# Token order by the second exp, whole-tile output transfers, and one batch loaded by half its heads

## The chip, the cores and the metric

The kernel runs on one core of a Trainium2 chip. The metric is device time in microseconds; the time before is 251.23 us, the median of three runs from 250.75 to 251.34. The core has a matrix engine (TensorE, PE in the profile, with its weight loads as PEld), a vector engine (VectorE, DVE), an activation engine (ScalarE, ACT), GpSimd (POOL) and SyncE (SP). POOL and SP issue most of the transfers here. Matrix results land in PSUM; everything else on the chip lies in SBUF.

## The reference

Eight batches, eight heads, 576 tokens, head size 64. A short set p of 32 rows a head attends to all keys and values; its result, the packed rows, serves as keys and as values for the queries. Then comes a two-layer network on the 4,608 tokens.

```python
def _attn_ref(q, k, v, p):
    scale = 1.0 / np.sqrt(q.shape[-1])
    def sm_attn(qq, kk, vv):
        s = scale * np.matmul(qq, kk.transpose(0, 1, 3, 2))
        s = s - np.max(s, axis=-1, keepdims=True)
        a = np.exp(s)
        a = a / (np.sum(a, axis=-1, keepdims=True) + 1e-09)
        return np.matmul(a, vv)
    p_packed = sm_attn(p, k, v)
    return sm_attn(q, p_packed, p_packed)

def _moe_ref(x, w_in, w_out):          # x: (4608, 512), w_in: (512, 2048), w_out: (2048, 512)
    h = x @ w_in
    g = np.where(h >= 1, h, np.where(h <= -1, 0.0, (h + 1) ** 2 / 4))
    return g @ w_out
```

## The kernel before

**Steps of a batch.** The names in brackets are the profile's. k and q are loaded with 96 partitions, each holding six successive tokens: token 6p + c lies in partition p, place c. c is written as 2e + x, with e from 0 to 2 and x 0 or 1. Both are turned, so that head size and x lie in the partitions and the columns run over e and then p. Batches 0 to 2 are turned by PE and an eviction (`trans`: tp, kT, qT), batches 3 to 7 by DMA transposes in SP's queue (`turned`, L512). Scores of p against k (`scores`: sp) go through an exp (ex), then products with v and sums (`packed`: pk), whose evictions (p, ppT, rs) leave the packed rows and the reciprocal sums. Queries against packed rows (`weights`: s) go through the second exp (eT, L456); its column sums (sm) are inverted by ln and exp (ln, rc), and DVE multiplies (A, L472). Both matmuls of A and of the hidden layer are merged: the packed rows are multiplied with w_in ahead of time (`mk`: mp, then M by a cast), four quarters a batch, and a hidden tile (`hidden_tile`: h, L548) is M times A, 128 hidden units by 576 tokens, 16 tiles a batch. Three steps on ACT and DVE make the activation (x, then hT). An output tile (`out_tile`: o, L598) is 128 tokens by 512, 16 steps over the hidden units; two batches share nine output tiles. It is evicted (ob) and sent out from SP's queue (L604), the last one in two halves from ACT's and SP's queues (L612).

**The order of tokens.** The columns of A, hT and so of the output tiles run over x, e and p, not in the order of the tokens. `out_rows` cuts a tile where e, x or the batch changes, and each piece goes to every sixth row of the output:

```python
n = min(TP - r, (i + 1) * P - t)
res.append((t - i * P, n, out[b * S:(b + 1) * S].rearrange("(p c) d -> c p d", c=NC)[X * e + x, r:r + n]))
```

**What sets the order of the work.** `Plan` (a list of tasks with costs, keys and dependencies) is run once when the program is written: it plays the engines through with the times in `C` and gives each engine a fixed order. The loads have one order of their own, that in which they were added (POOL's queue). `C["load"]` is the planned time of one load of a batch (288 KB halves cost `half`), and `C["xland"]` what passes between a DMA transpose and its landing. The actual engines then follow that order and wait on semaphores. PSUM has three wide buffers ("W") and two for output tiles ("O"). Until the plan has its first output tiles open, PE's gaps are filled with matmuls on zeros (L661).

**The loads.** Batch 0 comes by halves of the heads; then the four quarters of w_in and of w_out, with batch 1 ahead of the last w_out quarter; then p for the later batches and the batches 2 to 7 in turn. Of batch 1, k and q come in halves and v whole. Packing is done by halves of the heads (two calls of `packed`) in batch 0 alone; in the other batches it is one step for all heads.

Of the kernel before, what the change touches and what calls it, by code (L numbers as in the profile page):

```python
# [8 lines left out]

C = dict(load=2.95, half=1.46, w_in=2.57, w_out=2.57, rest=1.25, out=9.0, p=4.05, land=1.75, xt=5.0, xland=11.0,
         tpp=0.06, tp=0.042, sc=0.034, pk=1.05, s2=0.25, sm=0.245, M=0.345, h=0.49, o=0.217, switch=0.05, join=0.15,
         pTc=0.1, Tca=1.12, Tcd=0.76, ex=0.82, ppT=0.42, ppo=0.41, ppa=0.4, ppd=0.2, rs=0.18, eT=0.74, ln=0.65, rc=0.68, A=0.82,
         Mca=1.0, Mcd=1.22, x=0.65, ta=0.683, td=0.457, hT=0.758, oba=0.585, obd=0.69,
# [17 lines left out]
class Plan:  # L33
# [15 lines left out]
    def add(self, engines, cost, key, deps, fn, takes=None, readers=0, frees=None, mode=None, slack=None, after=0.0,  # L49
            holds=0.0):  # L50
        engines = (engines,) if isinstance(engines, str) else engines
        t = Task(engines, cost if isinstance(cost, dict) else {e: cost for e in engines}, key, deps, fn, takes, readers,
                 frees, mode, slack, after, holds)
        t.seq = len(self.tasks)
        self.tasks.append(t)
        return t
# [124 lines left out]
def kernel(  # L181
# [10 lines left out]
    nc = tc.nc  # L192
    f32 = mybir.dt.float32
    bf16 = mybir.dt.bfloat16
    AF = mybir.ActivationFunctionType
    ALU = mybir.AluOpType

    B, H, S, D = q.shape
# [3 lines left out]
    P = 128  # L202
    assert d_model == H * D and n_tokens == B * S
    assert S == 576 and D == 64 and NP == 32 and H == 8 and d_ff == 2048 and B % 2 == 0
    scale = 1.0 / math.sqrt(D)
# [3 lines left out]
    G = 2  # L209
    Q = 4  # L210
    TP = 96
    NC = S // TP
    X = 2
    E = NC // X
    HALF = S // X
    KF = d_ff // P
    FW = 512
    NF = d_ff // FW
# [15 lines left out]
    PE, ACT, DVE, DMA, SP = "PE", "ACT", "DVE", "DMA", "SP"  # L234
# [42 lines left out]
    def add_load(nm, b, parts=1, deps=(), cost="load"):  # L277
        for i, hs in enumerate([ALL] if parts == 1 else HS):
            L[nm, b, i] = add(DMA, C[cost] / parts, -1, deps, lambda nm=nm, b=b, hs=hs: load(nm, b, hs))
        if parts == 1:  # L280
            L[nm, b, 1] = L[nm, b, 0]

    def add_weights(which, f):
        if which == "in":
            fn = lambda: nc.gpsimd.dma_start(w_in_sb[:, :, f * FW:(f + 1) * FW], w_in_v[:, :, f * FW:(f + 1) * FW])  # L285
        else:
            fn = lambda: nc.gpsimd.dma_start(w_out_sb[:, 4 * f:4 * f + 4], w_out_v[:, 4 * f:4 * f + 4])
        L[which, f] = add(DMA, C["w_" + which], -1, (), fn)
# [8 lines left out]
            load(nm, 0, HS[i])  # L297
    for nm, i in FIRST:
        L[nm, 0, i] = add(DMA, C["half"], -1, (), (lambda: None) if L else first_loads)
    add_weights("in", 0)  # L300
    add_weights("in", 1)
    add_weights("out", 0)
    add_weights("in", 2)
    add_weights("out", 1)
    add_weights("in", 3)
    add_weights("out", 2)
    add_load("k", 1, 2)
    add_load("v", 1, 1)
    add_load("q", 1, 2)
    add_weights("out", 3)  # L310
    L["p"] = add(DMA, C["rest"], -1, (), lambda: nc.gpsimd.dma_start(p_nat[:, PB * 2:], p_v[:, PB * 2:]))


# [43 lines left out]
    def attention(b, key):  # L357
# [46 lines left out]
        def packed(gs, deps):  # L404
            box, ky = {}, key["pk" + str(gs[0])]
            hs, n = slice(Q * gs[0], Q * gs[-1] + Q), Q * len(gs)
            part = 0.55 if len(gs) < G else 1.0

            def mm():
                pk = wide([P, 1024], f32, "pk")  # L410
                vt, ex_ = tok["v", b], ex()
                v_ = box["v"] = pk[:, :n * X * NP].rearrange("p (h y) -> p h y", h=n)
                for g in gs:
                    for a in range(Q):
                        h = head(g, a)
                        for e in range(E):
                            nc.tensor.matmul(v_[:, h - hs.start].rearrange("p (x n) -> p x n", x=X),  # L417
                                             vt[:, h, X * e:X * (e + 1)].rearrange("p c d -> p (c d)"), ex_[:, e, g, :, a],
                                             start=(e == 0), stop=(e == E - 1))
                s_ = box["s"] = pk[:, 512:512 + 2 * len(gs)].rearrange("p (g y) -> p g y", y=2)  # L420
                for i, g in enumerate(gs):
                    for c in range(NC):
                        nc.tensor.matmul(s_[:, i], ex_[:, c // X, g, c % X].rearrange("p a n -> p (a n)"), ones2[:TP],  # L423
                                         start=(c == 0), stop=(c == NC - 1))
            t = add(PE, C["pk"] * len(gs) / G, ky, [L["v", b, g] for g in gs] + deps + old("s2", "M", "A"), mm, takes="W",
                    readers=3, mode=0)
            war = old("s2", "M")

            def odd(eng):
                box["p1"] = att.tile([D, n, NP], f32, tag="p1", name="p1")  # L430
                copy(box["p1"], box["v"][D:, :, NP:])(eng)
            c1 = both(odd, C["ppo"] * part, C["ppo"] * part, ky, [t] + war, frees=t)
            c2 = add(DVE, C["ppT"] * part, ky, [c1] + war, lambda eng: nc.vector.tensor_tensor(
                ppT()[:D, hs], box["v"][:D, :, :NP], box["p1"], ALU.add), frees=t)
            res = [c2, both(lambda eng: copy(ppT()[D:, hs], ppT()[:D, hs])(eng), C["ppa"] * part, C["ppd"] * part, ky, [c2] + war)]
            r = add(DVE, C["rs"], ky, [t] + old("eT", "A"), lambda eng: nc.vector.reciprocal(
                rs()[:, gs[0]:gs[-1] + 1], box["s"]), frees=t)
            return t, res, r
# [4 lines left out]
        def weights(g, deps, r):  # L443
            box, ky, km = {}, key["s2" + str(g)], key["sm" + str(g)]

            def mm():
                s2 = box["s2"] = wide([P, X, FW], f32, "s2")
                for a in range(Q):
                    h = head(g, a)
                    for x in range(X):  # L450
                        nc.tensor.matmul(s2[a * NP:(a + 1) * NP, x, :HALF], pp_of(x, h),  # L451
                                         qT()[x * D:(x + 1) * D, g, h % 4 * E * TP:][:, :E * TP], start=True, stop=True)

            def exp2(eng):
                box["eT"] = att.tile([P, X, HALF], bf16, tag="eT", name="eT")
                nc.scalar.activation(box["eT"], box["s2"][:, :, :HALF], AF.Exp, scale=rs()[:, g, 1:])  # L456

            def mm2():
                sm = box["sm"] = wide([P, X, FW], f32, "sm")
                for x in range(X):  # L460
                    nc.tensor.matmul(sm[:, x, :HALF], onesblk, box["eT"][:, x], start=True, stop=True)  # L461

            def ln(eng):
                box["ln"] = att.tile([P, X, HALF], f32, tag="ln", name="ln", bufs=1)
                nc.scalar.activation(box["ln"], box["sm"][:, :, :HALF], AF.Ln)  # L465

            def inv(eng):
                box["rc"] = att.tile([P, X, HALF], f32, tag="rc", name="rc")
                nc.scalar.activation(box["rc"], box["ln"], AF.Exp, scale=-1.0)  # L469

            def norm(eng):
                nc.vector.scalar_tensor_tensor(A()[:, g], box["eT"], rs()[:, g, :1], box["rc"], ALU.mult, ALU.mult)  # L472
            p_ = K.get((b - 1, "A" + str(g)), [])
            t, j = yield ky, C["s2"], deps + p_, mm
            e_ = add(ACT, C["eT"], ky, [t, r] + p_, exp2, frees=(t, j))
            t2 = add(PE, C["sm"], km, [e_], mm2, takes="W", readers=1, mode=0)
            l_ = add(ACT, C["ln"], km, [t2] + last.get("ln", []), ln, frees=t2)
            i_ = add(ACT, C["rc"], km, [l_] + p_, inv)
            a_ = add(DVE, C["A"], km, [i_] + K.get((b - 2, "h"), []), norm)
            last["ln"] = [i_]  # L480
            K[b, "A" + str(g)] = [a_]
            yield t, e_, a_
# [39 lines left out]
        s1, e1 = scores(1, kc1 + pT_of[b])  # L522
        q0, qc0 = trans("q", 0, qT, old("s2"))
        q1, qc1 = trans("q", 1, qT, old("s2"))
        pk, pc, r = zip(*([packed((0,), [e0]), packed((1,), [e1])] if b == 0 else [packed((0, 1), [e0, e1])] * G))
        K[b, "sc"], K[b, "pk"] = [s0, s1], list(pk)
        K[b, "kt"], K[b, "qt"] = [k0, k1], [q0, q1]
        ws, ms = [weights(g, pc[g] + (qc0, qc1)[g], r[g]) for g in range(G)], [mk(f, pc[0] + pc[1]) for f in range(NF)]
# [44 lines left out]
    def out_rows(pr, i):  # L573
        res, t = [], i * P
        while t < (i + 1) * P:
            b, x, e, r = 2 * pr + t // S, t % S // HALF, t % HALF // TP, t % TP
            n = min(TP - r, (i + 1) * P - t)
            res.append((t - i * P, n, out[b * S:(b + 1) * S].rearrange("(p c) d -> c p d", c=NC)[X * e + x, r:r + n]))
            t += n
        return res  # L580

# [54 lines left out]
    keys = {0: {nm: -1 + 0.01 * i for i, nm in enumerate(names)}}  # L636
    for f in range(1, NF):
        keys[0]["M" + str(f)] = 0.25 * f - 0.12
    order = "kT0 kT1 sc0 qT0 sc1 qT1 pk0 s20 M0 s21 sm0 M1 sm1 M2 M3".split()
    for b in range(1, B):  # L640
        lo, hi = (b - 1 + 0.05, b - 0.05)
        keys[b] = {nm: lo + (hi - lo) * i / len(order) for i, nm in enumerate(order)}
# [49 lines left out]
```

## Time and profile before

| | |
|---|---|
| median of three runs | 251.23 us (250.75 to 251.34) |
| the profiled execution | 250.97 us |
| its span in the profile | 249.2 us |
| PE busy | 234.8 us (94%) |
| DVE, ACT busy | 181.7 us, 182.5 us (73% each) |
| POOL busy | 29.7 us |
| output transfers at L604 | 70, of 192, 128 and 64 KB |
| chain that ended last | PE 76%, DMA 13%, ACT 3% |

The span is what the profile saw between the first and the last event on the core; the device time of the same execution is 1.8 us longer. Busy shares are means over a run whose stages differ: the beginning is fed by loads, the middle and the end are not. A row of the stretches gives start and end, length, then busy time and count of PE, PEld, DVE, ACT and POOL, the granted clock, the mean share of the DMA engines, and GB/s. A row of a timeline gives start, length, engine, line, operation and tiles, and in brackets the idle time ahead of it and what ended that. A row of a group gives the line, engine, operation, shapes and count, then busy time and mean ns of one, then idle time ahead of the group. A DMA row gives what was moved, the queue, the size, and the time from issue to landing.

### The profile page before, as it was taken

Reading aid. Unit: us, or ns where it says so; the run is one execution under the profiler, and the core shown is the slowest. Engines: PE = TensorE matmul, PEld = TensorE weight load, DVE = VectorE, ACT = ScalarE, POOL = GpSimd, SP = SyncE. Lnnn points to the kernel's source line nnn. Section 1 sums busy time; section 2 is a strip of 40 time slices with the busy share of each in tenths; the row PEclk is TensorE's granted clock in tenths of the full one; section 3 lists DMA queues with packets and bytes.
Section 4 is the critical chain, followed back from the end, with each engine's and each line's share of the span. In section 5 each row is a group of like instructions: output and inputs, shape, how many; then the busy total and the mean of one; then the engine's idle time right before and its main releaser. Section 6 shows DMA issues by size and latency. Waiting matters only on the chain.

```text
span 249.2 us, 5464 instructions
## 1 busy us (share of the span) xinstructions
PE 234.8 (94%) x2187; PEld 140.9 (57%) x2220; DVE 181.7 (73%) x308; ACT 182.5 (73%) x294; POOL 29.7 (12%) x44
## 2 busy tenths in 40 slices
PE   7887887999999999999999999999999999999993
PEld 5655465467546666556565656656556465544452
DVE  5456979788999899698979985998569878930000
ACT  3368888899888899798798984997859796841110
POOL 8632433012001301111101000000000000000000
PEclk9999999999999999999999999999999999999999
DMA  6999999999999999999999932312112112133223
GB/s 99 196 207 207 206 203 195 204 240 204 193 182 217 165 190 193 208 183 188 223 191 223 218 76 53 79 42 49 42 42 45 43 42 45 42 84 86 54 74 84
DMA packets 54825, 34.37 MB, mean 138 GB/s; under 512 B 27536, under 2 KB 50320, under 8 KB 54800
## 3 DMA queue, kind: packets, MB, share of 16 engines
q0 software_dynamic: 24672, 18.55, 49.9%
q1 hardware_dynamic: 29968, 15.34, 31.7%
q8 instruction: 17, 0.28, 0.4%
q10 hardware_dynamic: 160, 0.13, 0.2%
q14 instruction: 8, 0.07, 0.1%
HBM read 37.22 MB, written 9.44 MB: 187 GB/s over the span
## 4 chain that ended last, share of the span: by engine, by line
PE 76%; DMA 13%; ACT 3%; POOL 3%; issue 2%; DVE 2%; DVEq 0%; ACTq 0%; POOLq 0%
PE o L598 44%; PE h L548 22%; DMA w_in_sb<-in_moe_w_in_dram 7%; DMA q<-in_q_dram 6%; PE mp L493 3%; PE sp L397 2%; PE pk L417 1%; PE sm L461 1%; PE s L451 1%; PE tp L376 1%; DVE pT L319 1%; POOL w_in_sb L285 1%; ACT eT L456 1%; POOL k L259 1%; PE pk L423 1%
## 5 line engine op out<-in xcount | busy, mean ns | idle before, releaser
L598 PE MATMUL o<-w_out_sb,hT 128*128 128x512 bf16 (+1 forms) x559 | 135.6, 373 | 2.1 <-issue 1.1
L563 DVE SCALAR_TENSOR_TENSOR hT<-x 128x576 bf16<-128x576 f32 x128 | 93.2, 754 | 8.3 <-PE o L598 3.5
L598 PEld LDWEIGHTS <-hT 128*128 128x128 bf16 x592 | 56.1, 98 | 53.7 <-issue 4.8
L553 ACT ACTIVATE x<-h 128x576 f32<-128x576 f32 x128 | 77.2, 653 | 12.1 <-PE h L548 8.3
L548 PE MATMUL h<-A,M 128*128 128x288 bf16 x512 | 76.0, 286 | 1.4 <-ACT M L319 0.5
L548 PEld LDWEIGHTS <-M 128*128 128x128 bf16 x512 | 49.3, 98 | 24.1 <-ACT M L319 1.0
L558 DVE TENSOR_SCALAR x<-x 128x576 f32<-128x576 f32 x84 | 38.5, 459 | 11.8 <-ACT x L553 10.9
L319 ACT COPY ob<-o 128x512 f32<-128x512 f32 (+1 forms) x23 | 13.2, 576 | 32.1 <-PE o L598 32.1
L560 ACT ACTIVATE x<-x 128x576 f32<-128x576 f32 x44 | 29.4, 683 | 0.5
L319 DVE COPY ob<-o 128x512 f32<-128x512 f32 (+1 forms) x14 | 9.4, 669 | 25.8 <-PE o L598 25.7
L319 DVE CAST M<-mp 128x1024 bf16<-128x1024 f32 x16 | 19.4, 1218 | 2.8 <-PE mp L493 2.8
L319 ACT CAST M<-mp 128x1024 bf16<-128x1024 f32 x16 | 15.8, 1012 | 1.2 <-PE mp L493 1.2
L400 ACT ACTIVATE ex<-sp 96x768 bf16<-96x768 f32 x16 | 12.9, 806 | 3.2 <-PE sp L397 3.1
L472 DVE SCALAR_TENSOR_TENSOR A<-eT,rs,rc 128x576 bf16<-128x576 bf16 x16 | 13.0, 812 | 2.1 <-ACT rc L469 2.1
L259 POOL DMA_DIRECT2D k<-in_k_dram x10 | 7.5, 746 | 56.5 <-DMA kT<-k 40.0
L456 ACT ACTIVATE eT<-s,rs 128x576 bf16<-128x576 f32 x16 | 11.2, 736 | 2.8 <-PE s L451 2.6
L493 PE MATMUL mp<-w_in_sb,ppT 64*32 64x512 bf16 x256 | 10.7, 381 | 2.6 <-DMA w_in_sb<-in_moe_w_in_dram 2.2
L465 ACT ACTIVATE ln<-sm 128x576 f32<-128x576 f32 x16 | 10.4, 648 | 2.2 <-PE sm L461 2.1
L661 PE MATMUL o<-zeros 128*128 128x256 bf16 x68 | 10.6, 301 | 1.2 <-DVE zeros L247 1.2
L469 ACT ACTIVATE rc<-ln 128x576 f32<-128x576 f32 x16 | 10.9, 683 | 0.5
L259 POOL DMA_DIRECT2D q<-in_q_dram x10 | 7.6, 759 | 26.2 <-DMA qT<-q 12.7
L397 PEld LDWEIGHTS <-kT 128*128 128x128 bf16 x192 | 7.4, 98 | 2.6 <-DVE kT L319 0.6
(47 smaller groups left out, 114.4 us busy)
## 6 DMA issues: line engine op xcount, KB each, us to landing
out_dram<-ob SPq DMA_DIRECT2D x23, 192.0 KB, 2.5
v<-in_v_dram POOLq DMA_DIRECT2D x7, 576.0 KB, 18.4
k<-in_k_dram POOLq DMA_DIRECT2D x6, 576.0 KB, 12.4
q<-in_q_dram POOLq DMA_DIRECT2D x6, 576.0 KB, 14.0
out_dram<-ob SPq DMA_DIRECT2D x24, 128.0 KB, 2.8
w_in_sb<-in_moe_w_in_dram POOLq DMA_DIRECT2D x4, 512.0 KB, 14.7
w_out_sb<-in_moe_w_out_dram POOLq DMA_DIRECT2D x4, 512.0 KB, 16.8
out_dram<-ob SPq DMA_DIRECT2D x23, 64.0 KB, 2.0
```

The lines of the kernel that those rows point to most:

```text
L259: nc.gpsimd.dma_start(tok[nm, b][:, hs].rearrange("p h c d -> p h (c d)"), SRC[nm][b, hs].rearrange("h (p c) d -> p h (c d)", c=NC))
L319: return lambda eng: nc.vector.tensor_copy(out_, in_) if eng == DVE else nc.scalar.copy(out_, in_)
L400: nc.scalar.activation(ex()[:, :, i].rearrange("p e x a n -> p e (x a n)"), box["sp"], AF.Exp, scale=scale)
L456: nc.scalar.activation(box["eT"], box["s2"][:, :, :HALF], AF.Exp, scale=rs()[:, g, 1:])
L472: nc.vector.scalar_tensor_tensor(A()[:, g], box["eT"], rs()[:, g, :1], box["rc"], ALU.mult, ALU.mult)
L493: nc.tensor.matmul(mp[a * NP:(a + 1) * NP, g], pp_of(y, h), w_in_sb[y * D:(y + 1) * D, h // 2, f * FW:(f + 1) * FW], start=True, stop=True)
L548: nc.tensor.matmul(h[:, hf, :HALF], T[b, "M"][:, g, fi * P:(fi + 1) * P], T[b, "A"][:, g, hf], start=(g == 0), stop=(g == G - 1))
L553: nc.scalar.activation(box["x"], box["h"][:, :, :HALF], AF.Prelu, bias=-1.0, alpha=0.5)
L558: nc.vector.tensor_scalar(x, x, 1.0, 0.0, ALU.add, ALU.max)
L560: nc.scalar.activation(x, x, AF.Relu, bias=1.0)
L563: nc.vector.scalar_tensor_tensor(hT[:, fi, col:col + S].rearrange("p (a t) -> p a t", a=2), box["x"], 1.0, box["x"], ALU.min, ALU.mult)
L598: nc.tensor.matmul(o, hT[:, fi, i * P:(i + 1) * P], w_out_sb[:, fi, cs], start=(fi == 0), stop=(fi == KF - 1))
```

## The change

Four things are changed. First, the second exp writes its result in the order of the tokens in all batches: it reads PSUM as before and writes each value six elements from the one before it. So A, hT and the output tiles are in token order, and an output tile goes out as one transfer, or two where it holds the end of one batch and the beginning of the next. Second, v of batch 1 is loaded by halves of the heads as well, and the order of the loads between batch 0 and p is changed: three quarters of w_in, two of w_out, the first halves of k and v, the second half of k, the last quarter of w_in, the second half of v, the third quarter of w_out, both halves of q, the last quarter of w_out. Third, batch 1 is packed by halves of the heads like batch 0, and the list of keys has a place for the second half. Fourth, two planned times are changed: a load is 2.7 in place of 2.95, the landing of a transpose 18 in place of 11.

```diff
-C = dict(load=2.95, half=1.46, w_in=2.57, w_out=2.57, rest=1.25, out=9.0, p=4.05, land=1.75, xt=5.0, xland=11.0,
+C = dict(load=2.7, half=1.46, w_in=2.57, w_out=2.57, rest=1.25, out=9.0, p=4.05, land=1.75, xt=5.0, xland=18.0,
...
+    ORDERED = range(B)
...
-    add_weights("in", 0)
-    add_weights("in", 1)
-    add_weights("out", 0)
-    add_weights("in", 2)
-    add_weights("out", 1)
-    add_weights("in", 3)
-    add_weights("out", 2)
-    add_load("k", 1, 2)
-    add_load("v", 1, 1)
-    add_load("q", 1, 2)
-    add_weights("out", 3)
+    for nm in "i0 i1 i2 o0 o1 k0 v0 k1 i3 v1 o2 q0 q1 o3".split():
+        if nm[0] in "io":
+            add_weights({"i": "in", "o": "out"}[nm[0]], int(nm[1]))
+        else:
+            i = int(nm[1])
+            L[nm[0], 1, i] = add(DMA, C["half"], -1, (), lambda nm=nm, i=i: load(nm[0], 1, HS[i]))
...
-                nc.scalar.activation(box["eT"], box["s2"][:, :, :HALF], AF.Exp, scale=rs()[:, g, 1:])
+                eT, s2 = box["eT"], box["s2"][:, :, :HALF]
+                if b in ORDERED:
+                    eT = eT.rearrange("p y t -> p (y t)").rearrange("p (t e x) -> p x e t", x=X, e=E)
+                    s2 = s2.rearrange("p x (e t) -> p x e t", e=E)
+                nc.scalar.activation(eT, s2, AF.Exp, scale=rs()[:, g, 1:])
...
-        pk, pc, r = zip(*([packed((0,), [e0]), packed((1,), [e1])] if b == 0 else [packed((0, 1), [e0, e1])] * G))
+        pk, pc, r = zip(*([packed((0,), [e0]), packed((1,), [e1])] if b < 2 else [packed((0, 1), [e0, e1])] * G))
...
-            n = min(TP - r, (i + 1) * P - t)
-            res.append((t - i * P, n, out[b * S:(b + 1) * S].rearrange("(p c) d -> c p d", c=NC)[X * e + x, r:r + n]))
+            if b in ORDERED:
+                n = min(S - t % S, (i + 1) * P - t)
+                res.append((t - i * P, n, out[b * S + t % S:][:n]))
+            else:
+                n = min(TP - r, (i + 1) * P - t)
+                res.append((t - i * P, n, out[b * S:(b + 1) * S].rearrange("(p c) d -> c p d", c=NC)[X * e + x, r:r + n]))
...
-    order = "kT0 kT1 sc0 qT0 sc1 qT1 pk0 s20 M0 s21 sm0 M1 sm1 M2 M3".split()
+    order = "kT0 kT1 sc0 qT0 sc1 qT1 pk0 pk1 s20 M0 s21 sm0 M1 sm1 M2 M3".split()
```

## The prediction

> **What bounds the kernel now.** I read the page first, then the busy time by stretches, then TensorE's (PE's) timeline between 16 and 60 us, then the DMA landings, and last the chain that ended last.
>
> ```profile
> span 249.2 us, 5464 instructions
> PE 234.8 (94%) x2187; PEld 140.9 (57%) x2220; DVE 181.7 (73%) x308; ACT 182.5 (73%) x294; POOL 29.7 (12%) x44
> ...
> L661 PE MATMUL o<-zeros 128*128 128x256 bf16 x68 | 10.6, 301 | 1.2 <-DVE zeros L247 1.2
> ```
>
> PE is busy 234.8 of 249.2 us, but 10.6 us of that is the filler on zeros. So 224.2 us are real work, and 25.0 us are lost. The stretches, cut where something changes, tell where (the number after the comma is PE's busy time):
>
> ```profile
> 0.00:20.20 20.20, 16.24 (x214) 11.52 (x215) 10.17 (x26) 8.90 (x15) 12.10 (x22) 1.00 1.09 170
> 20.20:40.80 20.60, 17.79 (x200) 11.68 (x199) 17.10 (x30) 17.53 (x29) 6.43 (x9) 1.00 1.27 205
> 40.80:43.30 2.50, 1.87 (x38) 1.16 (x39) 2.47 (x4) 1.85 (x3) 1.46 (x2) 1.00 1.73 183
> 43.30:46.20 2.90, 2.34 (x34) 1.05 (x35) 2.17 (x3) 2.81 (x5) 0.07 (x1) 1.00 1.41 202
> 46.20:60.00 13.80, 13.40 (x168) 9.42 (x169) 11.76 (x19) 12.66 (x19) 1.87 (x3) 1.00 1.29 221
> 60.00:140.00 80.00, 78.95 (x757) 47.40 (x769) 71.49 (x120) 70.50 (x116) 7.79 (x10) 1.00 1.28 197
> 140.00:240.00 100.00, 98.91 (x748) 54.97 (x760) 66.15 (x109) 67.27 (x111) 0.00 (x0) 1.00 0.25 61
> 240.00:249.20 9.20, 5.27 (x40) 3.75 (x39) 0.42 (x1) 0.96 (x2) 0.00 (x0) 1.00 0.31 81
> ```
>
> Up to 20.2 us about 14.5 us are lost (3.96 idle and nearly all of the filler): PE waits for batch 0's tokens and the first part of w_in. From 20.2 to 46.2 it loses 2.81 + 0.63 + 0.56 = 4.0 us. From 46.2 to 240 us it loses only 0.40 + 1.05 + 1.09 = 2.5 us in 194, so there PE is the bound and nothing but less PE work helps. The last 9.2 us hold 3.9 us of tail. The clock was granted in full throughout (1.00). What the change can win lies therefore between 20 and 46 us and in the tail; what it can lose lies anywhere, since PE has hardly any slack behind 46 us.
>
> In the stretch from 20 us on, PE waits for loads. These are landings; in the timeline rows the bracket names what the engine waited for. The last two rows of the chain are for later:
>
> ```profile
> 19.20 0.41 PE L493 MATMUL mp<-w_in_sb,ppT 64*32 64x512 bf16 x8 [0.55 <-DMA w_in_sb<-in_moe_w_in_dram]
> 25.07 0.41 PE L493 MATMUL mp<-w_in_sb,ppT 64*32 64x512 bf16 x8 [0.98 <-DMA w_in_sb<-in_moe_w_in_dram]
> 33.59 0.68 PE L376 MATMUL tp<-ident,k 96*128 96x96 bf16 x12 [0.51 <-DMA k<-in_k_dram]
> ```
> ```profile
> 25.31 15.51 DMA q<-in_q_dram
> ...
> 96.09 1.47 PE h L548 x12
> ...
> 173.49 0.98 PE h L548 x8
> ```
> ```profile
> 27.25 0.75 POOL L287 DMA_DIRECT2D w_out_sb<-in_moe_w_out_dram  x1 [1.28 <-DMA w_out_sb<-in_moe_w_out_dram]
> ```
> ```profile
> w_out_sb<-in_moe_w_out_dram POOLq DMA_DIRECT2D x1, 512.0 KB, 16.1
> ```
>
> The second quarter of w_in is there at 19.2, the third at 25.0, batch 1's first half of k at 33.6, its last half of q at 25.31 + 15.51 = 40.8, the last quarter of w_out at 27.25 + 16.1 = 43.35. Until that last one, no output tile can be finished, and only two are open at a time (two PSUM buffers), each with 12 of its 16 steps: 24 steps. After it PE has 40 steps of output tiles 0 to 3 and batch 1's hidden tiles, and runs full.
>
> **The change part by part.**
>
> *Order of the loads.* The same bytes stand ahead of the last half of q and ahead of the last quarter of w_out, so these land at 40.8 and 43.35 as now; I cost that at nothing, and this is the main reason why the gain is small. Between 19.2 and 25.0 two pieces landed, 2.9 us each; the third quarter of w_in is now the first of them, so it comes at about 22.1. From 25.07 to 33.59 landed three pieces and a half-sized one, 8.5 / 3.5 = 2.4 us a piece; k's first half now stands ahead of two more pieces and comes 4.9 us sooner, at 28.7, v's first half 1.4 later, k's second at 31.5. The last quarter of w_in comes some 4 us later, at about 33.7. Who waits for that: batch 0's last four hidden tiles. They are covered: ACT and DVE, which each hidden tile needs, have 17.5 and 17.1 busy of 20.6 us in that stretch, and the early parts of batch 1 fill their queue meanwhile; and steps 12 to 15 of the output tiles wait for the last w_out quarter anyway. If that cover is gone, four hidden tiles (0.49 us of PE each, as in the row of three at 96.09) slip behind 43.3 us and cost up to 2.0 us, which is more than this part wins.
>
> *Packing batch 1 by halves.* Packed keys then are ready after v's second half, at about 35 us, and so the four products M of batch 1 can run before q lands. Now three of the four stand behind it (first and last of the three shown):
>
> ```profile
> 43.57 0.41 PE L493 MATMUL mp<-w_in_sb,ppT 64*32 64x512 bf16 x8 [0.29 <-DVE M L319]
> 45.05 0.38 PE L598 MATMUL o<-w_out_sb,hT 128*128 128x512 bf16 x1 [0.16 <-issue]
> 45.55 0.41 PE L493 MATMUL mp<-w_in_sb,ppT 64*32 64x512 bf16 x8
> 46.24 2.97 PE L598 MATMUL o<-w_out_sb,hT 128*128 128x512 bf16 x13
> 49.05 0.65 PE L548 MATMUL h<-A,M 128*128 128x288 bf16 x4
> ```
> ```profile
> L493 PE MATMUL mp<-w_in_sb,ppT 64*32 64x512 bf16 x256 | 10.7, 381 | 2.6 <-DMA w_in_sb<-in_moe_w_in_dram 2.2 <-DVE M L319 0.3
> L319 ACT COPY p<-pk 64x256 f32<-64x256 f32 x6 | 2.2, 368 | 2.0 <-PE pk L423 1.9
> L319 ACT COPY p<-pk 64x128 f32<-64x128 f32 x2 | 0.5, 262 | 2.0 <-PE pk L423 2.0
> ```
>
> 32 such groups of eight take 10.7 us, 0.33 each, so 1.0 us of PE work moves ahead of the last landing, into time that PE idles in now (0.63 us at 40.8 to 43.3, 2.81 before). With it goes part of the 0.56 us of idle at 43.3 to 46.2, which is made by the row of M copies that PE waits on there. Together 1.0 to 1.5 us; I take 1.2. PE's matmuls for packing stay the same number. What is added is small evictions: two of 262 ns for one of 368, and likewise for the three others of a pack, by the same proportion some 0.6 us of ACT and DVE in all; hidden in their 3 us of slack each in 20.2 to 40.8. One more load goes into POOL's queue (0.7 us), which waits for room there in any case. Bounds of both parts together: -1.5 (all of it) to +1.0 (hidden tiles slip, gain lost).
>
> *The second exp writes in token order.* It still reads PSUM in a straight line, 576 numbers; it writes bf16 at a step of six elements, 12 bytes. No instruction of this trace writes so. The nearest rows:
>
> ```profile
> L456 ACT ACTIVATE eT<-s,rs 128x576 bf16<-128x576 f32 x16 | 11.2, 736 | 2.8 <-PE s L451 2.6
> L319 ACT COPY ob<-o 128x512 f32<-128x512 f32 x22 | 12.9, 585 | 29.3 <-PE o L598 29.3
> L319 ACT COPY qT<-tp 128x1152 bf16<-128x1152 bf16 x3 | 3.4, 1118 | 0.2 <-PE tp L376 0.2
> L319 ACT COPY pT<-tpp 64x768 bf16<-64x768 bf16 x1 | 0.8, 795 | 0.3 <-DVE pT L319 0.3
> ```
>
> The two straight copies give (1118 - 585) / 640 = 0.83 ns an element, in bf16 and f32 alike; the pT copy, which writes runs of 32 elements with gaps between, lies on that line (585 + 256 x 0.83 = 798 against 795). So a write with gaps costs nothing there, and I take 0 for each of the 16. The upper end is an element at half rate: 576 x 0.83 = 480 ns more. I see no way for a gain. What follows (sums, A, hidden tiles) reads in a straight line as before.
>
> [...]
>
> *Output transfers.* 70 issues at L604 become 39 (eight whole tiles and one in two parts per pair of batches, less the last tile). None of them is on the path: PE does not wait for one. Two are, at the end:
>
> ```profile
> 245.36 0.42 DVE L319 COPY ob<-o 128x256 f32<-128x256 f32 x1 [24.50 <-PE o L598]
> 245.81 0.79 SPq L612 DMA_DIRECT2D out_dram<-ob  x2
> ```
> ```profile
> out_dram<-ob SPq DMA_DIRECT2D x1, 96.0 KB, 2.1
> ...
> out_dram<-ob SPq DMA_DIRECT2D x1, 32.0 KB, 2.0
> ```
>
> The second issue follows 0.4 us after the first and lands last, at about 248.2; a single one lands at 245.81 + 2.1 = 247.9. I take -0.3 us (0, if 128 KB take longer by as much, to -0.4). In SP's queue the transposes for batches 3 to 7 stand between the output transfers; fewer of these lets them go sooner, into time where they are waited for by later loads only.
>
> *The planner's constants.* It now believes that a load takes 2.7 and a transpose 7 us longer to land, so scores of batches 3 and up are placed later in PE's order.
>
> ```profile
> 61.73 5.86 SPq L512 DMA_TRANSPOSE kT<-k  x1
> ```
> ```profile
> kT<-k SPq DMA_TRANSPOSE x1, 16.4
> ```
> ```profile
> 79.01 0.51 PE L397 MATMUL sp<-pT,kT 128*128 128x64 bf16 x12
> ```
> ```profile
> 94.76 0.81 DVE L472 SCALAR_TENSOR_TENSOR A<-eT,rs,rc 128x576 bf16<-128x576 bf16 x1
> ```
>
> Batch 3's second transpose really lands at 78.1, 0.9 us ahead of its use at 79.0, so the old order was near a stall and the new one is farther from it. Batch 3's weights A are ready only at 94.76 + 0.81 = 95.57, 16.6 us behind those scores, so a shift of 7 us has room. I cost it at 0, with -0.3 to +1.5, since any other order of a full PE can stall somewhere.
>
> The sum: -1.2 - 0.3 = -1.5 us. The profiled execution took 250.97 us (span 249.2 and 1.8 around it), which gives 249.5; the median of the runs shown, 251.23, lies 0.26 above it, so I forecast 249.7.
>
> **The rivals.** (1) *The strided exp runs at half rate: slower.* A pair of them then ends 0.96 us later, and ACT's chain of two exps, ln, exp, ln, exp hands that on to A. How far A stands ahead of the batch's first hidden tile, for batch 3 (A until 95.57, the tile at 96.09) and for batch 6 (the tile at 173.49, A in this row):
>
> ```profile
> 172.49 0.82 DVE L472 SCALAR_TENSOR_TENSOR A<-eT,rs,rc 128x576 bf16<-128x576 bf16 x1 [0.58 <-ACT rc L469]
> ```
>
> 0.52 and 0.18 us. So PE would stand still 0.44 to 0.78 us in each of batches 3 to 7, 2.2 to 3.9 us; with the gains above, 251.9 to 253.6, and I name 252.4. It decides from about 0.33 us a piece: five stalls of 0.66 less a margin of 0.35 eat the 1.5 us. Against it: the pT row, whose gaps cost nothing; for it: that row's runs are 32 elements long, and here each element stands alone.
>
> (2) *The gain of the loads is hidden anyway.* PE's order for 40 to 50 us comes out such that the 1.0 us of M products was filling gaps that then stay empty, since the last landings do not move. Then only the tail is left: 250.9. For it: PE already idles 0.63 of the 2.5 us between the last two landings, so there is little else to run. Against it: what runs there sooner needn't run behind it.
>
> (3) *The new order stalls PE*, by hidden tiles that slip behind the last w_in quarter or by attention of later batches placed too late: 1 to 2 us lost, nothing won, 252.0.
>
> (4) *More is won*: the wait of 0.98 us for w_in's third quarter goes and batch 1's hidden tiles start at 47 in place of 49 us, which takes some of the 2.5 us of idle behind 46: 248.5.
>
> **How the numbers follow.** Forecast 0.42, (1) 0.13, (2) 0.20, (3) 0.16, (4) 0.09. 0.3% is 0.75 us, about what a measurement of this kernel can tell from no change. Faster: 0.40 of the first and all of (4), with 0.03 of (2): 0.52. Same: the rest of (2), 0.02 of the first, 0.02 of (3): 0.21. Slower: 0.27. The forecast's own range is 249.0 to 250.5; 8 in 10 reach from 248.4 (case 4) to 252.6 (rivals 1 and 3 without their ends).
>
> **What would show it.** Right: the exp on L456 stays within 20 ns of 736; the group for batch 1's M stands ahead of 41 us; PE's idle from 40 to 46 us falls from 1.2 us below 0.7 with the last landing still near 43.3; two transfers at the tail, not four; idle from 46 to 240 stays near 2.5 us. Wrong: an exp near 1.2 us with PE waiting for A; hidden tiles of batch 0 after 43 us; PE rows that wait for kT, or for v of batch 2; the last landing later than 44.

## The result and the profile after

The changed kernel takes 268.44 us in the median (267.56 to 273.19), the kernel before 251.26 us: a ratio of 1.068, with a 95% interval of 1.064 to 1.072. It is 17 us slower, where 1.5 us less were forecast, and beyond the end of the range (252.6). The highest of the four times is a slow run at a lower granted clock, and the ratio leaves it out. The profiled execution took 268.93 us with a span of 267.1.

The page of the changed kernel, with the group of the second exp (now L457) and that of the column sums behind it; below, the column sums in the kernel before:

```profile
span 267.1 us, 5445 instructions
PE 243.7 (91%) x2220; PEld 142.1 (53%) x2220; DVE 180.1 (67%) x309; ACT 206.1 (77%) x297; POOL 29.7 (11%) x45
...
PE 68%; ACT 13%; DMA 12%; POOL 2%; DVE 2%; issue 2%; ACTq 0%; POOLq 0%
...
L457 ACT ACTIVATE eT<-s,rs 128x576 bf16<-128x576 f32 x16 | 33.4, 2231 | 2.7 <-PE s L447 2.6
...
L462 PE MATMUL sm<-eT,onesblk 128*128 128x288 bf16 x32 | 6.5, 283 | 14.7 <-ACT eT L457 14.7
```
```profile
L461 PE MATMUL sm<-eT,onesblk 128*128 128x288 bf16 x32 | 6.5, 286 | 0.2
```

The second exp takes 2,231 ns in place of 736, sixteen times 1.5 us or 24 us more of ACT. ACT's share of the chain that ended last went from 3% to 13%. PE's column sums, which had waited 0.2 us in all, now wait 14.7 us for the exp. The list of waits says the same from both ends:

```profile
DVE A L473 <- ACT rc L470: 19.0, 12, 3.2
...
PE sm L462 <- ACT eT L457: 14.7, 15, 1.3
```

The stretches of the changed kernel (start and end, length, busy time and count of PE, PEld, DVE, ACT, POOL, granted clock, DMA share, GB/s) show a loss that comes back with each batch:

```profile
60.00:80.00 20.00, 18.10 (x179) 10.08 (x178) 16.82 (x29) 17.57 (x24) 1.93 (x3) 0.91 1.31 180
80.00:100.00 20.00, 20.00 (x195) 12.44 (x193) 17.18 (x31) 17.94 (x30) 2.68 (x4) 1.00 1.35 165
100.00:120.00 20.00, 18.15 (x168) 10.45 (x167) 12.81 (x21) 16.45 (x24) 2.30 (x3) 0.91 1.22 173
...
180.00:200.00 20.00, 18.13 (x172) 9.79 (x171) 12.12 (x21) 15.73 (x21) 0.00 (x0) 1.00 0.11 41
```

Where a pair of exps lies, PE idles about 1.9 us of 20 in the stretches shown (1.5 to 2.1 in all six behind 60 us); where none lies, it is full. One such place, batch 2's, first in the chain and then on PE's timeline:

```profile
71.32 4.00 ACT eT L457 x2
```
```profile
71.38 1.25 PE L603 MATMUL o<-w_out_sb,hT 128*128 128x512 bf16 x5
73.45 0.41 PE L462 MATMUL sm<-eT,onesblk 128*128 128x288 bf16 x2 [0.82 <-ACT eT L457]
73.69 0.59 PE L603 MATMUL o<-w_out_sb,hT 128*128 128x512 bf16 x2
75.36 0.41 PE L462 MATMUL sm<-eT,onesblk 128*128 128x288 bf16 x2 [1.08 <-ACT eT L457]
75.61 2.96 PE L603 MATMUL o<-w_out_sb,hT 128*128 128x512 bf16 x7
```

PE's order was written for exps of 0.74 us: five output steps, the sums of the first half, two steps, the sums of the second. The steps run out, and PE stands twice for about a microsecond. The last row has something more: seven output steps take 2.96 us there, where seven took 1.68 us in the kernel before. The clock, by the microsecond:

```profile
73.00:74.00 1.00, 0.55 (x4) 0.38 (x4) 0.96 (x3) 1.00 (x2) 0.00 (x0) 1.00 1.29 190
74.00:75.00 1.00, 0.29 (x2) 0.01 (x1) 0.41 (x1) 1.00 (x2) 0.00 (x0) 1.00 1.30 184
75.00:76.00 1.00, 0.64 (x4) 0.41 (x4) 0.00 (x0) 0.97 (x3) 0.00 (x0) 0.92 1.91 195
76.00:77.00 1.00, 1.00 (x4) 0.30 (x2) 0.46 (x1) 0.97 (x2) 0.00 (x0) 0.50 1.21 35
...
79.00:80.00 1.00, 1.00 (x26) 0.28 (x11) 1.00 (x2) 0.80 (x1) 0.40 (x1) 0.88 1.29 168
```

After some two microseconds in which PE was less than half busy, its granted clock fell to 0.50 at about 75.8 and came back at 79.2 us. So a stall can be paid a second time, though not each one is: by the stretches above it happened here and between 100 and 120 us, and not between 180 and 200.

The loss can be added up from these figures, as an estimate. The two stretches at a clock of 0.91 lack 0.09 x 20 = 1.8 us of full clock each, 3.6 us together. With the 14.7 us of waits at the column sums that is 18.3 us; the span grew by 267.1 - 249.2 = 17.9 us.

### The profile page after: what moved, and what is told of

Read it like the earlier page. It is cut to its first block, busy times and chain, and to the rows that moved or that the text cites. A ratio compares the mean times of both kernels' runs of the same rounds, so it can differ in the third digit from the quotient of the medians.

```text
span 267.1 us, 5445 instructions
## 1 busy us (share of the span) xinstructions
PE 243.7 (91%) x2220; PEld 142.1 (53%) x2220; DVE 180.1 (67%) x309; ACT 206.1 (77%) x297; POOL 29.7 (11%) x45
## 4 chain that ended last, share of the span: by engine, by line
PE 68%; ACT 13%; DMA 12%; POOL 2%; DVE 2%; issue 2%; ACTq 0%; POOLq 0%
PE o L603 40%; PE h L549 20%; ACT eT L457 10%; DMA w_out_sb<-in_moe_w_out_dram 6%; DMA q<-in_q_dram 6%; PE mp L494 2%; PE pk L413 2%; PE sp L393 1%; ACT ob L315 1%; PE sm L462 1%; POOL w_in_sb L286 1%; PE tp L372 1%; PE pk L419 1%; DVE hT L564 1%; ACT pT L315 1%
## 5 line engine op out<-in xcount | busy, mean ns | idle before, releaser
L603 PE MATMUL o<-w_out_sb,hT 128*128 128x512 bf16 (+1 forms) x592 | 146.0, 379 | 0.6 <-ACT ob L315 0.3
L559 DVE TENSOR_SCALAR x<-x 128x576 f32<-128x576 f32 x89 | 41.3, 464 | 14.7 <-ACT x L554 14.1
L457 ACT ACTIVATE eT<-s,rs 128x576 bf16<-128x576 f32 x16 | 33.4, 2231 | 2.7 <-PE s L447 2.6
L315 DVE COPY ob<-o 128x512 f32<-128x512 f32 (+1 forms) x12 | 8.0, 666 | 28.2 <-PE o L603 28.1
L561 ACT ACTIVATE x<-x 128x576 f32<-128x576 f32 x39 | 26.3, 684 | 0.3
L462 PE MATMUL sm<-eT,onesblk 128*128 128x288 bf16 x32 | 6.5, 283 | 14.7 <-ACT eT L457 14.7
L315 DVE CAST M<-mp 128x1024 bf16<-128x1024 f32 x14 | 17.1, 1221 | 3.9 <-PE mp L494 3.6
L315 ACT CAST M<-mp 128x1024 bf16<-128x1024 f32 x18 | 17.6, 1012 | 1.7 <-PE mp L494 1.5
L462 PEld LDWEIGHTS <-onesblk 128*128 128x128 bf16 x32 | 3.1, 97 | 20.0 <-issue 18.4
L466 ACT ACTIVATE ln<-sm 128x576 f32<-128x576 f32 x16 | 11.9, 745 | 0.7 <-PE sm L462 0.6
```

Of the source, the lines that this page charges most:

```text
L315: return lambda eng: nc.vector.tensor_copy(out_, in_) if eng == DVE else nc.scalar.copy(out_, in_)
L457: nc.scalar.activation(eT, s2, AF.Exp, scale=rs()[:, g, 1:])
L559: nc.vector.tensor_scalar(x, x, 1.0, 0.0, ALU.add, ALU.max)
L561: nc.scalar.activation(x, x, AF.Relu, bias=1.0)
L603: nc.tensor.matmul(o, hT[:, fi, i * P:(i + 1) * P], w_out_sb[:, fi, cs], start=(fi == 0), stop=(fi == KF - 1))
```

## The experiments

Twelve kernels ran, each compared with the kernel before on the same chip (one of them is the kernel before itself, and one a probe).

**Which part of the change costs.** All of the change but the token order:

```diff
-    ORDERED = range(B)
+    ORDERED = ()
```

> All of the change but the token order (the second exp writes straight again, pieces go out as before). Theory A, the write at a step of 12 bytes is the whole loss: the exp is back at 736 ns and the time is the forecast without the tail's 0.3 us, 250.0 us (249.3 to 251). Rival B, the new order of loads, packing and the planned landing of 18 cost as well: 253 us or more, with waits of PE that the kernel before doesn't have.

Measured: 251.38 us, ratio 0.999 (0.996 to 1.001), the exp at 740 ns. The exp is back as theory A has it, but the time is above its range: the gain that it counted on is not seen. The token order alone, put into the kernel before:

```diff
-                nc.scalar.activation(box["eT"], box["s2"][:, :, :HALF], AF.Exp, scale=rs()[:, g, 1:])
+                eT = eT.rearrange("p y t -> p (y t)").rearrange("p (t e x) -> p x e t", x=X, e=E)
+                s2 = s2.rearrange("p x (e t) -> p x e t", e=E)
+                nc.scalar.activation(eT, s2, AF.Exp, scale=rs()[:, g, 1:])
...
-            n = min(TP - r, (i + 1) * P - t)
+            n = min(S - t % S, (i + 1) * P - t)
```

> Only the token order (second exp and whole-tile transfers) put into the kernel before. Theory A: exp 2.2 us, 16 x 1.5 us on ACT, PE waits for it at the column sums, 266 to 270 us. Rival B: a part of the 17 us stays away, 256 to 262 us.

Measured: 269.74 us, ratio 1.072 (1.067 to 1.076), the exp at 2,232 ns. So the token order is the whole loss.

**Is it the order, or the side on which it is made?** The changed kernel with the steps moved to the read:

```diff
-                    eT = eT.rearrange("p y t -> p (y t)").rearrange("p (t e x) -> p x e t", x=X, e=E)
-                    s2 = s2.rearrange("p x (e t) -> p x e t", e=E)
+                    eT = eT.rearrange("p y t -> p (y t)").rearrange("p (t e x) -> p t e x", x=X, e=E)
+                    s2 = s2.rearrange("p x (e t) -> p t e x", e=E)
```

> The changed kernel, but the second exp reads PSUM in the order of the tokens (steps of 512 and 96 f32) and writes straight. Theory A, the step on the write side is what costs: exp 736 to 790 ns, 249.7 us (249 to 250.7). Rival C, the three-level pattern or any broken-up access costs, on whichever side: exp above 1.2 us, 255 us or more.

Measured: 251.02 us, ratio 0.998 (0.996 to 0.999). The group of the exp:

```profile
L457 ACT ACTIVATE eT<-s,rs 128x576 bf16<-128x576 f32 x16 | 11.3, 740 | 2.8 <-PE s L447 2.6
```

The same permutation costs 4 ns when PSUM is read in steps of 384 bytes and 2 KB and SBUF is written straight. All else of the change is in this kernel too, and with it the kernel is faster than the one before, by a quarter of a percent; 249.7 us, which were expected, were not reached.

**What a broken-up write costs.** A probe runs exps and copies alone; it computes nothing of the reference.

```python
for nm, dt, k in [("w1", bf16, 1), ("w2", bf16, 2), ...]:      # four of each
    t = const.tile([P, N * k], dt, name=nm)
    nc.scalar.activation(t.rearrange("p (n k) -> p n k", k=k)[:, :, 0], src, AF.Exp, scale=0.5)
```

> Exps and copies alone, 576 elements from PSUM each, four of a kind, output all zeros: bf16 written at steps of 1, 2, 3, 4, 6, 7, 8, 16 elements (w1 to w16), f32 at 1, 2, 3, 4, 6 (f1 to f6), the change's pattern (perm), the same on the read side (rperm), pairs of bf16 at 24 bytes (pairs), SBUF read at step 6 (r6), VectorE copies written at 1, 2, 6 (d, df, dperm). [...] Rival C: w6 near 740 ns and only perm and rperm slow.

The profile leaves numbers out of tile names, so the kinds are told apart by their order in time. Rows from narrow windows of the probe's timeline, for bf16 at 2, 4, 6, 8, 12 and 16 bytes (a row of two joins neighbouring instructions; the time of one is then the distance between starts, which is 0.03 us more than its own length), and its groups:

```profile
3.47 1.33 ACT L214 ACTIVATE w<-src 128x576 bf16<-128x576 f32 x2
...
6.60 0.81 ACT L214 ACTIVATE w<-src 128x576 bf16<-128x576 f32 x1
...
11.16 1.16 ACT L214 ACTIVATE w<-src 128x576 bf16<-128x576 f32 x1
...
17.56 1.52 ACT L214 ACTIVATE w<-src 128x576 bf16<-128x576 f32 x1
...
24.50 4.19 ACT L214 ACTIVATE w<-src 128x576 bf16<-128x576 f32 x2
26.61 4.19 ACT L214 ACTIVATE w<-src 128x576 bf16<-128x576 f32 x2
...
42.88 5.46 ACT L214 ACTIVATE w<-src 128x576 bf16<-128x576 f32 x2
45.63 5.46 ACT L214 ACTIVATE w<-src 128x576 bf16<-128x576 f32 x2
```

```profile
L214 ACT ACTIVATE f<-src 128x576 f32<-128x576 f32 x20 | 18.1, 936 | 0.5
L219 ACT ACTIVATE perm<-src 128x576 bf16<-128x576 f32 x4 | 8.3, 2086 | 0.1
...
L223 ACT ACTIVATE rperm<-src 128x576 bf16<-128x576 f32 x4 | 2.8, 702 | 0.1
L227 ACT ACTIVATE pairs<-src 128x576 bf16<-128x576 f32 x4 | 2.7, 670 | 0.1
```
```profile
99.14 4.15 DVE L240 CAST d<-src 128x576 bf16<-128x576 f32 x2
101.23 4.17 DVE L240 CAST d<-src 128x576 bf16<-128x576 f32 x2
```

| step of the write | 2 B | 4 B | 6 B | 8 B | 12 B | 14 B | 16 B | 24 B | 32 B |
|---|---|---|---|---|---|---|---|---|---|
| bf16, us for 576 | 0.68 | 0.81 | 1.16 | 1.52 | 2.11 | 2.43 | 2.75 | | 2.60 |
| f32, us for 576 | | 0.68 | | 0.71 | 0.96 | | 1.21 | 1.20 | |

The values without a row here are read in the same way; those of f32 have the mean 0.95, against 936 ns in the group's row.

The time rises with the step up to 16 bytes and no farther: bf16 takes 2.75 us at 16 bytes and 2.60 at 32, f32 1.21 at 16 and 1.20 at 24. f32 is nearly free at 8 bytes (0.71 against 0.68 us straight), bf16 is dearer at 4 bytes already (0.81 against 0.68). An estimate from the table: at 16 bytes, less 0.2 us of fixed time (worked out below), 2.55 us / 576 = 4.4 ns a number for lone bf16 numbers and 1.0 / 576 = 1.75 ns for f32, and at shorter steps as much less as the step is shorter. At 12 bytes that is 0.2 + 576 x 0.75 x 4.4 ns = 2.1 us, as measured, and 0.2 + 576 x 0.75 x 1.75 = 0.96 us for f32. A straight element's 0.83 ns, from the two copies in the prediction, is the least; 576 x 0.83 = 0.48 us leaves the fixed 0.2 of the 0.68. Pairs of bf16, 4 bytes every 24, are 288 pieces; at 4.4 ns that would be 0.2 + 1.27 = 1.47 us, at the price of f32 0.2 + 0.50 = 0.70, and 0.67 is measured. So it is not bf16 that is dear but two bytes written alone, by 2.5 times (4.4 against 1.75 ns). Perm, the change's own pattern, is as slow as a plain step of 12 bytes (2,086 ns against 2.08 us, a row's own length), and rperm, the same pattern on the read side, is not slow (702 ns): rival C falls. DVE takes the same 2.1 us for bf16 at 12 bytes (101.23 - 99.14), so the price is not ACT's alone; what makes it was not shown.

A read of SBUF at this step is not free either. The exp with bf16 from SBUF, straight and then at 12 bytes a step, both written straight:

```profile
7.25 0.68 ACT L234 ACTIVATE r<-sb 128x576 bf16<-128x576 bf16 x1
...
13.80 0.99 ACT L234 ACTIVATE r<-sb 128x576 bf16<-128x576 bf16 x1
```

Both stand between scattered writes of the probe, whose ends they overlap, so the price is rough. It is the read from PSUM that cost nothing here (740 ns against 736).

**Is it ACT's time, or does the write hold up others?** The kernel with the read-side order, with two discarded exps ahead of each second one:

```diff
+                spare = att.tile([P, X, HALF], bf16, tag="spare", name="spare")
+                for _ in range(2):
+                    nc.scalar.activation(spare, box["s2"][:, :, :HALF], AF.Exp, scale=rs()[:, g, 1:])
```

> The kernel with the read-side order, with two more exps of the same input ahead of each second exp, written straight into a spare tile that nobody reads: some 2.1 us of ACT in place of 0.74, with no scattered write. Theory, it is ACT's time in the chain to A that costs: 265 to 269 us, PE waiting for the exp at the column sums, the clock falling after such waits. Rival, the scattered write also takes SBUF from other engines: 260 us or less.

Measured: 269.00 us, ratio 1.070 (1.066 to 1.073).

```profile
L459 ACT ACTIVATE spare<-s,rs 128x576 bf16<-128x576 f32 x32 | 23.7, 741 | 3.2 <-PE s L447 2.6
...
L460 ACT ACTIVATE eT<-s,rs 128x576 bf16<-128x576 f32 x16 | 11.7, 732 | 0.0
```
```profile
PE sm L465 <- ACT eT L460: 15.6, 15, 1.6
```

As much ACT time without any scattered write costs the same 17 us, and PE waits at the same place (15.6 us against 14.7). Nothing beside ACT's time has to be assumed.

**How much was the plan's not knowing?** The changed kernel, told of it:

```diff
-         pTc=0.1, Tca=1.12, Tcd=0.76, ex=0.82, ppT=0.42, ppo=0.41, ppa=0.4, ppd=0.2, rs=0.18, eT=0.74, ln=0.65, rc=0.68, A=0.82,
+         pTc=0.1, Tca=1.12, Tcd=0.76, ex=0.82, ppT=0.42, ppo=0.41, ppa=0.4, ppd=0.2, rs=0.18, eT=2.2, ln=0.65, rc=0.68, A=0.82,
```

> The changed kernel, with 2.2 in place of 0.74 as the planned time of the second exp. Theory: 24 us more of ACT with 90% of its time taken between 20 and 150 us cannot all be hidden, but the waits of PE at the column sums can be filled with other steps: 256 to 262 us. Rival: the plan cannot help, 266 us or more; or the whole loss was the plan's not knowing, 252 us or less.

Measured: 256.88 us, ratio 1.022 (1.017 to 1.027), with the exp as slow as ever:

```profile
L457 ACT ACTIVATE eT<-s,rs 128x576 bf16<-128x576 f32 x16 | 33.2, 2238 | 6.6 <-PE s L447 6.6
```
```profile
PE sm L462 <- ACT eT L457: 1.5, 2, 1.0
```

Two thirds of the loss (268.4 to 256.9, 11.5 of 17 us) was the order of PE, which had too few steps between an exp and its sums; the waits there fall from 14.7 to 1.5 us. The other 5.6 us stay. Most of them lie between 40.8 and 60 us, where PE idles 1.34 + 2.67 = 4.0 us (1.6 in the kernel before) and the clock falls once more, to 0.88 in the mean of this stretch:

```profile
46.20:60.00 13.80, 11.13 (x103) 7.17 (x103) 9.68 (x16) 11.92 (x19) 0.77 (x1) 0.88 1.31 204
```

**What the loads, the packing and the transfers do.** The token order by the read, put into the kernel before, without the new loads:

```diff
-                nc.scalar.activation(box["eT"], box["s2"][:, :, :HALF], AF.Exp, scale=rs()[:, g, 1:])
+                eT = eT.rearrange("p y t -> p (y t)").rearrange("p (t e x) -> p t e x", x=X, e=E)
+                s2 = s2.rearrange("p x (e t) -> p t e x", e=E)
+                nc.scalar.activation(eT, s2, AF.Exp, scale=rs()[:, g, 1:])
...
-            n = min(TP - r, (i + 1) * P - t)
+            n = min(S - t % S, (i + 1) * P - t)
```

> The kernel before with token order alone, taken on the read side of the second exp, and whole-tile transfers; its loads, packing and planned times. Theory: what the changed loads win in the kernel with the read is nothing, the 0.25% come from the two transfers fewer at the end, so this gives the same: 250.7 us (250.3 to 251.0), last transfers 0.3 us sooner. Rival: the loads did win something that is hidden in the noise: then 251.2 us.

Measured: 250.80 us, ratio 0.999 (0.997 to 1.001). The transfers alone thus don't clear the noise either. New loads and packing without token order and with the old planned times:

```diff
-    ORDERED = range(B)
+    ORDERED = ()
...
-C = dict(load=2.7, half=1.46, w_in=2.57, w_out=2.57, rest=1.25, out=9.0, p=4.05, land=1.75, xt=5.0, xland=18.0,
+C = dict(load=2.95, half=1.46, w_in=2.57, w_out=2.57, rest=1.25, out=9.0, p=4.05, land=1.75, xt=5.0, xland=11.0,
```

> The new order of loads and the packing of batch 1 by halves alone: no token order, planned load and landing as in the kernel before. Theory: the two planned times change nothing that the loads don't, so 251.3 us (250.9 to 251.7), like all of the change but the token order. Rival: loads and planned times offset one another, and this is 250.3 us or less, or 252 us or more.

Measured: 252.00 us, ratio 1.002 (1.000 to 1.005), above the range of the theory and at the bound of the rival. Neither this nor the transfers alone differs clearly from the kernel before; between all but the token order (0.999) and this, the planned times may win 0.3%, but the intervals overlap. The transfers' part can be read off the end: from the start of the last DVE copy to the end of the span it was 249.2 - 245.36 = 3.84 us before; with one transfer a half, in the kernel with the read, 249.0 - 245.58 = 3.42:

```profile
245.58 0.42 DVE L315 COPY ob<-o 128x256 f32<-128x256 f32 x1 [24.50 <-PE o L603]
```

That is 0.4 us won (0.3 forecast). The front part was to win 1.2 us. PE in the kernel without token order, and then in the kernel before, where the last of the two stretches was not yet shown:

```profile
40.80:46.20 5.40, 5.40 (x62) 2.47 (x61) 5.30 (x9) 5.19 (x8) 1.53 (x2) 1.00 1.56 192
46.20:52.00 5.80, 5.06 (x57) 3.09 (x50) 3.71 (x5) 5.11 (x8) 0.77 (x1) 1.00 1.27 235
```
```profile
46.20:52.00 5.80, 5.45 (x51) 3.33 (x50) 4.71 (x7) 4.80 (x8) 0.00 (x0) 1.00 1.29 218
```

The 1.2 us of idle at 40.8 to 46.2 are gone as forecast; but then PE idles 0.74 us in place of 0.35. Not all of it went as forecast: of batch 1's four products M, two run ahead of 41 us (at 38.77 and 40.18 in the kernel without token order), the third at 41.99, and the last behind the sums:

```profile
45.87 0.41 PE L494 MATMUL mp<-w_in_sb,ppT 64*32 64x512 bf16 x8
```

Batch 1's A comes later. In the kernel before it ended at 46.25 + 0.82 = 47.07 us:

```profile
46.25 0.82 DVE L472 SCALAR_TENSOR_TENSOR A<-eT,rs,rc 128x576 bf16<-128x576 bf16 x1 [0.25 <-ACT rc L469]
```

In the kernel with the read it ends at 48.15 + 0.82 = 48.97, and the first hidden tile comes at 51.03 in place of 49.05:

```profile
45.77 1.07 ACT L315 COPY ob<-o 128x512 f32<-128x512 f32 x2
...
48.15 0.82 DVE L473 SCALAR_TENSOR_TENSOR A<-eT,rs,rc 128x576 bf16<-128x576 bf16 x1
```
```profile
51.03 1.83 PE L549 MATMUL h<-A,M 128*128 128x288 bf16 x12 [0.52 <-DVE kT L315]
```

Three attempts at the reason failed. First: the last w_in quarter comes too late.

```diff
-    for nm in "i0 i1 i2 o0 o1 k0 v0 k1 i3 v1 o2 q0 q1 o3".split():
+    for nm in "i0 i1 i2 i3 o0 k0 v0 k1 v1 o1 o2 q0 q1 o3".split():
```

> The kernel with the read-side order, the loads being w_in whole, one quarter of w_out, k and v of batch 1 by halves, two quarters of w_out, q, the last quarter of w_out. Theory: the last quarter of w_in came too late in the changed order, batch 0's last hidden tiles kept DVE until 45 us, M's cast and with it the PSUM buffer for the column sums came late, and A with it: now A of batch 1 is ready by 47 us in place of 49, and the time is 249.7 us (249.2 to 250.3). Rival: the end of this stretch is set by the last landings whatever the order: 251.0 us, as with the read alone.

Measured: 255.40 us, ratio 1.015 (1.013 to 1.018). With w_out later, PE lacked steps:

```profile
20.20:40.80 20.60, 16.12 (x202) 10.37 (x199) 14.47 (x27) 16.36 (x27) 7.02 (x10) 1.00 1.27 205
```

It idles 4.5 us there, against 2.8 in the kernel before and 2.65 in the one with the read. Second: the evictions of the first two output tiles, which PE finishes sooner, stand on ACT in the middle of the chain to A (the row at 45.77).

```diff
+        if pr == 0 and i < 2:
+            add(DVE, C["obd"], b_key(pr, i), prev, done, frees=owner, takes="ob", holds=C["out"])
+            return
```

> The kernel with the read-side order, with the evictions of the first two output tiles kept on DVE. Theory: the 8 output steps that PE does sooner end two output tiles at 45.8 us, whose evictions (2 x 0.58 us) then stand on ACT between the first and the second half of batch 1's chain to A; without them A is ready by 48 us in place of 49, PE's gap of 0.5 us at 50.5 goes, and the time falls to 250.2 us (249.8 to 250.7). Rival: A's place is set by PSUM buffers and by the exps themselves; then 251.0 us as before, or slower by what DVE has more.

Measured: 250.97 us, ratio 0.998 (0.996 to 0.999), the same as without it. A came no sooner (47.48 + 1.54 = 49.02), and PE stood for another eviction:

```profile
47.48 1.54 DVE L473 SCALAR_TENSOR_TENSOR A<-eT,rs,rc 128x576 bf16<-128x576 bf16 x2
```
```profile
51.52 0.66 PE L549 MATMUL h<-A,M 128*128 128x288 bf16 x4 [0.55 <-DVE pT L315]
```

Third: the chain from q is what holds the stretch.

```diff
-    for nm in "i0 i1 i2 o0 o1 k0 v0 k1 i3 v1 o2 q0 q1 o3".split():
+    for nm in "i0 i1 i2 o0 i3 k0 v0 k1 v1 q0 q1 o1 o2 o3".split():
```

> The kernel with the read-side order, with q of batch 1 loaded ahead of all but one of the w_out quarters (its last half lands near 36.6 us in place of 40.8; the last w_out quarter last, as before). Theory: batch 1's hidden tiles can start some 3 us sooner and fill PE after the last landing, but up to 39 us only eight output steps can run, so PE idles more before: 251 us (250 to 252). Rival, the chain from q to A is what holds the stretch: 249.5 us or less.

Measured: 256.28 us, ratio 1.020 (1.017 to 1.023): both statements too low; PE's idle at 20.2 to 40.8 rose to 4.8 us.

Last, the kernel before a second time, for a fuller record (only a comment is added):

> The kernel before once more, unchanged, for a second record: in the first one 33 of the 592 output matmuls are missing, and its idle times count them as idle. Theory: with fuller records PE idles 1.1 to 1.2 us at 40.8 to 46.2 us as before, and 0.3 us or less from 60 to 245 us (2.2 us in the first record); then PE was full behind 60 us all along. Rival: 2 us of idle are there again.

Its one time is 251.31 us. The record has as many output matmuls missing (33), PE idles 1.5 us at 40.8 to 46.2, and behind 60 us as much as in the first, 1.05 us from 60 to 140. Since the records are not fuller, this run doesn't test the theory. The first record does. Two rows from the end of its chain:

```profile
219.22 10.74 PE o L598 x49
230.01 10.74 PE o L598 x49
```

From the start of one row to that of the next it is 10.79 us, which is 50 steps of 0.216 us; 49 are recorded, and a gap of 0.05 us stands in place of the one that is missing. All but 0.09 of the 2.1 us of idle from 60 to 240 us in the kernel before lies in gaps of 0.05 and 0.16 us, and the kernel with the read, whose record lacks no matmul, has no gap of either length. So PE was full from 60 to 240 us, as the theory has it. One gap of 0.16 us also stands at 40.8 to 46.2 (the row at 45.05 in the prediction), so that about 1.0 us of real idle was to be won there.

## Why the prediction was wrong

**The second exp: the step that failed.** The prediction took 0 ns, with half rate (480 ns) as the upper end. It measured 1,495 ns. The value came from the wrong row: the pT copy writes runs of 64 bytes, and its 795 ns say nothing of a write in which every two bytes stand alone. The upper end was wrong for the same reason: nothing in the trace bounded it, and half rate was only a guess. What the prediction named for its first rival, that here each element stands alone, had the right sign.

**The first rival: right cause, wrong size and place.** It put the loss at twice the exp's excess less A's lead, 0.52 and 0.18 us, in each of batches 3 to 7. With the measured 1.495 us that is 2.5 to 2.8 us a batch, 12.4 to 14.0 in all, of the 17 measured. That this comes near is in part luck, since PE stood at another place: at the column sums ahead of A, where its order had too few steps, about 1.9 us a batch. The rival also left out batches 0 to 2 and the half clock after some stalls.

**The order of the loads and the packing.** The step "PE's idle falls" was right (1.2 us to none at 40.8 to 46.2 us), the step "and that is won" was not: the ratio is 0.999. Of the 1.2 us, 0.16 was a missing record and no idle; 0.4 us came back at 46.2 to 52, as a later A and as waits for evictions, and 0.2 us between 60 and 140 us. By the profiles some 0.4 us are left, which the interval of the ratio (0.3% to either side) cannot tell from nothing. One step under it failed: two of the four products M moved ahead of q, not all four. Why A comes later isn't settled. The second rival, that the gain of the loads would be hidden, is how this part came out, though for other reasons than it gave. The landings came as forecast: in the changed kernel PE gets the first half of k at 28.56 us (28.7 forecast) and the last quarter of w_in at 34.06 (33.7), and in the one without token order batch 0's last hidden tiles are done at 38.4, so that quarter did no harm where it was put. Both orders tried that had it sooner took 4.4 and 5.3 us more than the kernel with the read; they moved quarters of w_out back as well.

**The output transfers.** Right: two at the end, 0.4 us sooner (0.3 forecast), and nothing else on the path. The quarter of a percent that the kernel with the read wins is about of that size.

**The planner's constants.** Costed at 0; between 0.999 with them and 1.002 without, not to be told apart.

**"PE has hardly any slack behind 46 us".** Right, and more so than it said: of the 2.5 us of idle that it counted from 46 to 240 us, 2.1 us are missing records. It should have weighed more: of the 24 us by which sixteen exps grew, 17 came out in the time.

## What to carry to other kernels

If a permutation must be made, make it where PSUM is read, and write SBUF straight: the same exp took 740 ns in the one way and 2,231 in the other. A read of SBUF at such a step is a third case, and was dearer than a straight one (roughly, 0.99 against 0.68 us). A price from a row with gaps holds only for gaps of the same kind; for a scattered write take a row with its own step and width (bf16 in the probe: 0.68 us at 2 bytes, 2.11 at 12). Where an order is written out from planned times, a wrong planned time can cost more than the work itself: told of the slow exp, the plan hid two thirds of it.

## What the runs showed of the hardware

In the probe an exp of 576 numbers that ACT wrote to SBUF took longer with the step of the write up to 16 bytes: bf16 0.68 us at 2 bytes, 2.11 at 12, 2.75 at 16 and 2.60 at 32; f32 0.68 at 4, 0.96 at 12, 1.21 at 16 and 1.20 at 24. By the estimate above, a number at 16 bytes cost 1.75 ns in f32 and 4.4 ns in lone bf16, over 0.2 us, and a straight one 0.83 ns. Pairs of bf16 at 24 bytes took 0.67 us, no more than a straight write. DVE took the same 2.1 us as ACT for bf16 at the 12-byte step. A read of PSUM in steps of 384 bytes and 2 KB cost ACT next to nothing (740 ns against 736 in the kernel, 702 ns in the probe).

In the changed kernel TensorE's granted clock fell to 0.50 for 3.4 us, from about 75.8 us, after waits of 0.82 and 1.08 us within 2.7 us; in that time PE was busy in part, and not idle for longer than 1.1 us at a time. At a like pair of waits, 0.79 and 1.07 us before 184.22 and 186.13 us, it stayed at 1.00.
